# Attention and routed experts on one core: the attention part in a fixed order on every engine

## The chip, the cores and the metric

The kernel runs on one core of a Trainium2 chip. A core has several engines, each with its own stream of instructions: TensorE (PE, with its weight loads PEld), VectorE (DVE), ScalarE (ACT), GpSimd (POOL), and SyncE (SP), which here only issues transfers (DMA). An engine works through its stream in order; where an instruction needs what another engine or a transfer makes, it waits for a semaphore, and all that stands behind it in the same stream waits too.

The metric is the device time of a whole launch, in microseconds. The profile covers the span from the first to the last instruction of one execution, which is shorter than the launch.

## The reference

Two blocks follow one another. The first is attention over 4 batches, 8 heads, 768 positions and 64 features, with a mask: a query sees only keys whose 6 sign bits under a projection equal its own. The second sends each of the 3072 rows of 512 features to one of 8 experts, by cosine similarity, and gives gate times relu(x w1) w2.

```python
q_bits = (np.einsum('bhsd,dk->bhsk', q, proj) > 0)
k_bits = (np.einsum('bhsd,dk->bhsk', k, proj) > 0)
# buckets are the bits read as numbers
mask = q_bucket[:, :, :, None] == k_bucket[:, :, None, :]
scores = scale * np.matmul(q, k.transpose(0, 1, 3, 2))
scores = np.where(mask, scores, -1000000000.0)
attn = softmax(scores)
x = np.matmul(attn, v)            # then (B,H,S,D) -> (B*S, H*D)
...
logits = normed(x) @ normed(expert_emb).T / tau
expert_idx = np.argmax(logits, axis=1)
gate_w = softmax(logits)[expert_idx]
for e in range(E):
    h = np.maximum(x[mask_e] @ w1[e], 0.0)
    out[mask_e] = gate_w[mask_e, None] * (h @ w2[e])
```

## The kernel before

Attention works on 16 pairs of heads (4 batches of 4 pairs). A pair has 12 units: two halves s of the queries by 6 blocks c of keys. The loop takes three units at a time, so a pair is four steps, g = 0 to 3. A step makes the scores of three units and then the products with v of the three units before.

```python
def scores(u):
    ...
    ps = banks()                       # one of three PSUM buffers of two banks
    for h in range(2): nc.tensor.matmul(ps[:, h, 0:SH], lhsT=kt[...], rhs=qt[...], start=True, stop=False)
    for h in range(2): nc.tensor.matmul(ps[:, h, 0:SH], lhsT=kb[...], rhs=qb[...], start=False, stop=True)
    p = pts[u % NPT]                   # six buffers
    last[0] = nc.scalar.activation(p[:, :, 0:SH], ps[:, :, 0:SH], ACT.Exp, scale=ESCALE).ins
    if c == 1: ...                     # acc = p of unit 0 + p
    elif c > 1: last[1] = nc.vector.tensor_tensor(out=a[:], in0=a[:], in1=p[...], op=ALU.add).ins

def attend(u):                         # av += v^T p; after the last c:
    ...
    nc.scalar.copy(out=few[:], in_=ps[:, SH : SH + 1])
    nc.scalar.activation(xs(b)[:, j, ...], ps[:, 0:SH], ACT.Identity, bias=few[:])
```

The softmax's denominators of a pair are summed over partitions by TensorE (`sums`), go through DRAM twice to be laid out anew (za, zc, zd, rz), and are multiplied into x by GpSimd (`scale`). `store` writes x to DRAM, from where the expert part gathers rows; `add_squares` makes the norms; `prep_features` turns q and k, `prep_bits` makes the mask's features.

```python
def sums(pr):
    ps = banks()
    ...                                               # ones^T acc, eight matmuls
    nc.vector.tensor_scalar_add(z[:], ps[:, 0, 0:SH], TINY * S)
    nc.sync.dma_start(za[pr], z[0:P:32, :])
    nc.sync.dma_start(zc[:], za[pr]...)

def scale(pr):
    with tc.issue_after(last[1]):
        nc.vector.reciprocal(out=zc[:], in_=zc[:])
    nc.sync.dma_start(zd[pr]..., zc[:])
    for h in range(2): nc.sync.dma_start(rz[...], zd[pr]...)
    scaled[0] = nc.gpsimd.tensor_tensor(out=x, in0=x, in1=rz[...], op=ALU.mult).ins

def add_squares(pr, rp, ins):
    with tc.issue_after(ins):
        nc.scalar.activation(t[:], xs(b)[:, j], ACT.Square)
    if j > 0: nc.gpsimd.tensor_tensor(out=ssq[b][:], in0=ssq[b][:], in1=t[:], op=ALU.add)
```

The loop, with the order in which the program names the work. The framework then chooses each engine's order itself; `issue_after` and `high_priority` only steer it.

```python
for u0 in range(0, U + G, G):
    pr, g = u0 // PU, u0 % PU // G
    run(7 if pr == len(pairs) - 2 else 3)       # small steps of the placement of rows
    ...                                         # scores of three units
    if pr == len(pairs) - 2 and g == 3:
        lists(...); early = [fetch(src[0], pos[0], 0, 2, ZC + 1)]
    ...                                         # attend for the three units before
    if g == 0:
        prep_features(pr + 1, 0); add_squares(pr - 2, ...); sums(pr - 1); store(pr - 2)
        ...                                     # begin(b, ...) for the last batch but one
    elif g == 1:
        prep_features(pr + 1, 1)
        ...                                     # begin: counts for the placement
        scale(pr - 1)                           # in the last pair: behind the gathers
        ...                                     # last pair: fetch for the second expert
        square(pr)                              # sum of squares of q and k, for a bound check
        if j == 1 and b >= 0: lts[b] = logits(b, ...)
    elif g == 2:
        prep_bits(pr + 1); load(pr + 3)         # 8 loads of q and k, 1 of v
        ...                                     # fill, gates of the last batch but one
        if j == 1 and b >= 0: route(...)
    else:
        if pr == 2: prep_experts()              # loads, norms and turns the expert embeddings
        ...                                     # fill, gates
        if pr == 2 * NP:
            with tc.issue_after(loads[-1]): bring1(0, 0); bring2(0, 0)   # 2 MB each
early = [turn(got) for got in early]
store(len(pairs) - 2); scale_last(len(pairs) - 1); store(len(pairs) - 1)
...                                             # the bound check: largest square, turned and reduced
```

The expert part then begins with `hidden(0, early[0][0], 2 * P)`: 64 matmuls for rows of expert 0, in PSUM buffers that take the place of attention's.

Of the kernel before, what the change touches and what calls it, by code (L numbers as in the profile page):

```python
# [9 lines left out]
I32 = mybir.dt.int32  # L10
# [16 lines left out]
def kernel(  # L27
# [204 lines left out]
    def gates(b, rp):  # L232
        l, nrm = lts.pop(b)
        nc.vector.tensor_scalar_add(nrm[:], nrm[:], 1e-6)
        nc.vector.reciprocal(out=nrm[:], in_=nrm[:])
        nc.vector.tensor_tensor(out=l, in0=l, in1=nrm[:].unsqueeze(2).broadcast_to([P, NC, E]),
                                op=ALU.mult)
        nc.scalar.activation(l, l, ACT.Exp)
        g = rp.tile([P, NC], F32, name="g", tag="g")
        nc.vector.reduce_sum(out=g[:], in_=l, axis=AX.X)  # L240
        nc.vector.tensor_scalar_add(g[:], g[:], 1e-9)
        nc.vector.reciprocal(out=gate_all[:, b], in_=g[:])
        nc.sync.dma_start(gd[b * S : (b + 1) * S, :].rearrange("(p c) o -> p (c o)", c=NC), gate_all[:, b])
# [79 lines left out]
    def lists(slots, src, pos, n, ps, sp):  # L323
# [4 lines left out]
        nc.vector.tensor_scalar_add(src, tmp[:], float(N))  # L328
        for g in range(NQ):
            nc.tensor.matmul(ps[:, g * 2 * n : (g + 1) * 2 * n], lhsT=pick[:, g], rhs=half_[:].rearrange("p i t -> p (i t)"),  # L330
                             start=True, stop=True)
# [3 lines left out]
        return nc.vector.tensor_tensor(out=pos, in0=at[:], in1=t[:, :, :, 1], op=ALU.add).ins  # L335
# [11 lines left out]

    def bring2(i, e, **kw):
        nc.sync.dma_start(w2s[i][:], w2[bass.ds(e, 1)].rearrange("o (c p) m -> p (o c) m", p=P), **kw)

    xgs = [const.tile([P, NQ, P], F32, name=f"xg{i}") for i in range(4)]
    taken, copied = [0, 0, 0], [None]


    def fetch(src, pos, t, n, width=N + 1):
        parts = []
        for i in range(n):
            xg = xgs[taken[2] % len(xgs)]
            taken[2] += 1
            for g in range(NQ):  # L360
                copied[0] = nc.gpsimd.indirect_dma_start(  # L361
                    out=xg[:, g, :], out_offset=None, in_=xd[0 : width * NQ, :],
                    in_offset=bass.IndirectOffsetOnAxis(ap=pos[:, t + i, g : g + 1], axis=0)).ins
            parts.append(xg)
        tiles = []
        for i in range(n):
            g = ggs[taken[1] % len(ggs)]
            taken[1] += 1
            with tc.issue_after(copied[0]):
                nc.gpsimd.indirect_dma_start(out=g[:], out_offset=None, in_=gd[:, :],  # L370
                                             in_offset=bass.IndirectOffsetOnAxis(ap=src[:, t + i : t + i + 1], axis=0))
# [17 lines left out]
    def add_squares(pr, rp, ins):  # L389
# [4 lines left out]
        with tc.issue_after(ins):  # L394
            nc.scalar.activation(t[:], xs(b)[:, j], ACT.Square)
        if j > 0:
            return nc.gpsimd.tensor_tensor(out=ssq[b][:], in0=ssq[b][:], in1=t[:], op=ALU.add).ins
# [3 lines left out]

    with ExitStack() as at:
        ldp = pool("ldp", 3, at)
# [25 lines left out]


        def prep_experts():
            emb = const.tile([E, DM], F32, name="emb")
            nc.sync.dma_start(emb[:], expert_emb[:, :])
            tau_t = const.tile([E, 1], F32, name="tau_t")
            nc.sync.dma_start(tau_t[:], tau.unsqueeze(0).broadcast_to([E, 1]))
            sq = rp.tile([E, DM], F32, name="emb_sq", tag="junk", bufs=2)
            ss = const.tile([E, 1], F32, name="emb_ss")
            with tc.issue_after(last[0]):
                nc.scalar.activation(sq[:], emb[:], ACT.Square, accum_out=ss[:])
            nrm = const.tile([E, 1], F32, name="emb_nrm")  # L440
            nc.gpsimd.tensor_tensor(out=nrm[:], in0=ss[:], in1=half[0:E, 0:1], op=ALU.pow)
            nc.vector.tensor_scalar_add(nrm[:], nrm[:], 1e-6)
            nc.vector.reciprocal(out=nrm[:], in_=nrm[:])
            rtau = const.tile([E, 1], F32, name="rtau")
            nc.vector.reciprocal(out=rtau[:], in_=tau_t[:])
            nc.vector.tensor_scalar(out=emb[:], in0=emb[:], scalar1=nrm[:, 0:1], scalar2=rtau[:, 0:1],
                                    op0=ALU.mult, op1=ALU.mult)
            ps = banks()
            for d in range(ND):
                nc.tensor.transpose(ps[:, 0, d * E : (d + 1) * E], emb[:, d * P : (d + 1) * P], ident[0:E, 0:E])  # L450
            with tc.high_priority():
# [3 lines left out]
        def load(pr):  # L455
# [4 lines left out]
            vt = ldp.tile([P, 2, NC, D], F32, name="vt", tag="vt", bufs=3)  # L460
# [6 lines left out]
            loads.append(nc.sync.dma_start(vt[:], v[b, 2 * j : 2 * j + 2].rearrange("h (p c) d -> p h c d", c=NC)).ins)  # L467
# [10 lines left out]
        def square(pr):  # L478
            qk = ld[pr][0]
            sq = rp.tile([P, 2 * S], BF16, name="qksq", tag="junk", bufs=2)  # L480
            with tc.issue_after(last[0]):
                nc.scalar.activation(sq[:], qk[:].rearrange("p i n f -> p (i n f)"), ACT.Square,
                                     accum_out=squares[:, pr : pr + 1])
# [27 lines left out]
        def scores(u):  # L511
# [12 lines left out]
            last[0] = nc.scalar.activation(p[:, :, 0:SH], ps[:, :, 0:SH], ACT.Exp, scale=ESCALE).ins  # L524
# [4 lines left out]
            elif c > 1:  # L529
                a = acc[pr, s]  # L530
                last[1] = nc.vector.tensor_tensor(out=a[:], in0=a[:], in1=p[:, :, 0:SH], op=ALU.add).ins  # L531


        def spare(n):
            return last[2][:, SH + 1 : SH + 1 + n]

        def attend(u):
# [7 lines left out]
            if c == NC - 1:  # L545
# [4 lines left out]
                last[2] = av.pop((pr, s))  # L550
# [19 lines left out]
        def scale(pr):  # L570
            b, j = pairs[pr]
            zc = zcs.pop(pr)
            with tc.issue_after(last[1]):
                nc.vector.reciprocal(out=zc[:], in_=zc[:])
# [6 lines left out]
            scaled[0] = nc.gpsimd.tensor_tensor(out=x, in0=x, in1=rz[:].rearrange("p s n -> p (s n)"), op=ALU.mult).ins  # L581


        def store(pr):
            b, j = pairs[pr]
            t = op.tile([P, S], F32, name="xb", tag="xb")
            with tc.issue_after(last[1]):
                nc.vector.transpose(t[:], xs(b)[:, j])  # L588
# [6 lines left out]
        def scale_last(pr):  # L595
# [10 lines left out]
            for s in range(2):  # L606
# [3 lines left out]
                ins = nc.vector.tensor_tensor(out=z[:, s], in0=x, in1=x, op=ALU.mult).ins  # L610
            x = xs(b)[:, j - 1]
            with tc.issue_after(ins):
                nc.vector.tensor_tensor(out=t[:], in0=x, in1=x, op=ALU.mult)
                nc.vector.tensor_tensor(out=t[:], in0=t[:], in1=z[:].rearrange("p s n -> p (s n)"), op=ALU.add)
                nc.vector.tensor_tensor(out=ssq[b][:], in0=ssq[b][:], in1=t[:], op=ALU.add)

        last, loads, scaled = [None, None, None], [], [None]
        steps = []

        def run(n):  # L620
            for _ in range(n):
                if steps:
                    with tc.issue_after(last[1]):
                        if next(steps[0], None) is None:
                            steps.pop(0)

        def begin(b, ps):
            with tc.high_priority():
                count(b, ps[:, 0 : E * NC], ps[:, E * NC :])
                steps.append(place(b, ps.rearrange("p (t n) -> p t n", t=2), rp))  # L630
                next(steps[0])

        for pr in range(3):
            load(pr)
        for i in range(2):
# [3 lines left out]
        early = []  # L639
        for u0 in range(0, U + G, G):  # L640
            pr, g = u0 // PU, u0 % PU // G
            run(7 if pr == len(pairs) - 2 else 3)
# [418 lines left out]
```

## Time and profile before

The time is 872.76 us, the median of three launches (872.59 to 873.0). The profiled span is 818.3 us.

| | before |
|---|---|
| TensorE busy | 730.6 us (89%) |
| VectorE busy | 345.5 us (42%) |
| ScalarE busy | 267.8 us (33%) |
| GpSimd busy | 223.4 us (27%) |
| last matmul of attention ends | about 427 us |
| first matmul of the expert part | 438.94 us |

The page gives the busy share of each engine in 40 equal slices of the span. A digit is tenths, and 9 means 90% or more; PEclk is the clock that TensorE was granted, in tenths. In a list of waits, a line names the engine and the line of the program that waited, the one that it waited for, and then the total in microseconds, the number of times and the longest. In a timeline, a line gives start, length, engine, line, operation, output and inputs; what stands in brackets is the idle time before it and what ended that. An issue of a transfer has the engine SPq.

### The profile page before, as it was taken

The page shows a single profiled execution, that of the slowest core. Times are in us where ns is not written, and L with a number is a line of the kernel's source. Part 1 is how long each engine was busy: PE and PEld are TensorE (multiplying, and loading weights), DVE is VectorE, ACT ScalarE, POOL GpSimd, SP SyncE. Part 2 cuts the span into 40 slices and gives each one's busy share as a digit, 9 for nine tenths or more (in the row PEclk, how much of TensorE's full clock was granted, in tenths as well). Part 3 has the DMA queues.
Part 4 walks back from the last instruction along what each step waited for, and adds up shares of the span by engine and source line. Part 5 has one row for each costly group of instructions (what it writes and reads, how often), then busy time and mean ns, then how long its engine had stood idle before and what let it go on. Part 6 is the DMA issues. An engine that isn't in the chain of part 4 may idle for free.

```text
span 818.3 us, 9991 instructions
## 1 busy us (share of the span) xinstructions
PE 730.6 (89%) x3669; PEld 361.2 (44%) x3669; DVE 345.5 (42%) x664; ACT 267.8 (33%) x432; POOL 223.4 (27%) x222
## 2 busy tenths in 40 slices
PE   5997299898998999849865999999999999999993
PEld 2442143343443433314324576654545454545481
DVE  5765187688775787628555141151010101010100
ACT  3654176564565565535450111110101010101020
POOL 4000131101202102110443117777661522010051
PEclk9998599999999999978986999999999999999997
DMA  8313344335438234541325402944442433333340
GB/s 153 80 23 76 78 81 96 70 69 98 83 55 265 52 71 75 98 83 17 82 49 152 126 20 96 348 153 161 166 159 89 155 125 128 113 129 114 129 144 20
DMA packets 198075, 87.56 MB, mean 107 GB/s; under 512 B 171377, under 2 KB 179373, under 8 KB 198008
## 3 DMA queue, kind: packets, MB, share of 16 engines
q1 hardware_dynamic: 188312, 72.94, 34.6%
q0 software_dynamic: 6560, 13.41, 4.8%
q10 hardware_dynamic: 3136, 0.39, 0.3%
q8 instruction: 33, 0.54, 0.3%
q14 instruction: 34, 0.28, 0.1%
HBM read 82.31 MB, written 13.31 MB: 117 GB/s over the span
## 4 chain that ended last, share of the span: by engine, by line
PE 65%; DMA 9%; DVE 8%; issue 7%; POOL 4%; ACT 3%; SPq 2%; DVEq 0%; ACTq 0%; POOLq 0%
PE ps_h L867 21%; PE ps_y L875 20%; PE banks L518 9%; PE av L543 9%; DMA zd<-zc 4%; DVE acc L531 3%; DMA rz<-zd 3%; PE banks L521 2%; ACT p L524 2%; POOL xT L581 2%; PE banks L496 1%; POOL xg L361 1%; SPq L463 1%; SPq L578 1%; DVE kb L507 1%
## 5 line engine op out<-in xcount | busy, mean ns | idle before, releaser
L518 PE MATMUL banks<-qt,kt 64*128 64x384 f32 x768 | 174.2, 527 | 20.0 <-ACT p L524 9.6
L875 PE MATMUL ps_y<-w,ht 128*128 128x512 f32 x416 | 180.9, 593 | 0.0
L524 ACT ACTIVATE p<-banks 128x768 f32<-128x768 f32 x192 | 153.2, 811 | 78.9 <-PE banks L521 77.0
L869 ACT ACTIVATE ht<-ps_h 128x384 f32<-128x384 f32 (+2 forms) x96 | 38.6, 403 | 319.0 <-PE ps_h L867 317.6
L543 PE MATMUL av<-p,vt 128*64 128x385 f32 x768 | 142.4, 506 | 0.0
L531 DVE TENSOR_TENSOR acc<-acc,p 128x768 f32<-128x768 f32 x128 | 132.2, 1033 | 22.0 <-ACT p L524 11.7
L867 PE MATMUL ps_h<-xgt,w 128*128 128x384 f32 (+1 forms) x512 | 139.6, 434 | 0.0
L875 PEld LDWEIGHTS ps_y<-w,ht 128*128 128x128 f32 x416 | 78.5, 190 | 95.2 <-issue 93.3
L361 POOL DMA_INDIRECT xg<-xd,pos x96 | 93.2, 971 | 66.8 <-issue 25.0
L581 POOL TENSOR_TENSOR xT<-xT,rz 128x768 f32<-128x768 f32 x15 | 30.4, 2030 | 293.8 <-DMA rz<-zd 279.2
L867 PEld LDWEIGHTS ps_h<-xgt,w 128*128 128x128 f32 x512 | 87.4, 190 | 52.2 <-issue 2.9
L518 PEld LDWEIGHTS banks<-qt,kt 64*128 64x128 f32 x768 | 69.5, 195 | 92.4 <-issue 43.1
L543 PEld LDWEIGHTS av<-p,vt 128*64 128x64 f32 x768 | 50.8, 139 | 79.3 <-issue 78.3
L879 DVE TENSOR_SCALAR y<-ps_y,gg 128x512 f32<-128x512 f32 x26 | 19.3, 744 | 142.5 <-PE ps_y L875 140.1
L381 DVE STREAM_TRANSPOSE xgt<-xg 128x512 f32<-128x512 f32 x21 | 14.2, 699 | 139.7 <-PE ps_h L867 80.4
L521 PE MATMUL banks<-qb,kb 64*128 64x384 bf16 x384 | 67.2, 332 | 0.0
L880 POOL DMA_INDIRECT out_dram<-y,src x24 | 24.3, 1012 | 146.8 <-DVE y L879 104.8
L867 PE MATMUL ps_h<-xge,w 128*128 128x256 f32 (+1 forms) x256 | 45.8, 341 | 11.8 <-issue 11.8
L528 DVE TENSOR_TENSOR acc<-p,p 128x768 f32<-128x768 f32 x32 | 31.6, 988 | 40.8 <-ACT p L524 40.8
L867 PEld LDWEIGHTS ps_h<-xge,w 128*128 128x128 f32 x256 | 40.7, 199 | 16.9 <-issue 12.9
L521 PEld LDWEIGHTS <-kb 64*128 64x128 bf16 x384 | 20.8, 97 | 26.5 <-issue 3.0
L588 DVE STREAM_TRANSPOSE xb<-xT 128x768 f32<-128x768 f32 x16 | 15.6, 974 | 29.0 <-POOL xT L581 29.0
(241 smaller groups left out, 393.2 us busy)
## 6 DMA issues: line engine op xcount, KB each, us to landing
w<-in_moe_w_dram SPq DMA_DIRECT2D x24, 2048.0 KB
qk<-in_q_dram SPq DMA_DIRECT2D x64, 96.0 KB
vt<-in_v_dram SPq DMA_DIRECT2D x16, 384.0 KB
xd<-xb SPq DMA_DIRECT2D x64, 96.0 KB
qk<-in_k_dram SPq DMA_DIRECT2D x60, 96.0 KB
rz<-zd SPq DMA_DIRECT2D x30, 192.0 KB
xg<-xd,pos POOLq DMA_INDIRECT x96, 2.8
qk<-in_k_dram ACTq DMA_DIRECT2D x4, 96.0 KB
```

What stands on the lines that cost most here:

```text
L361: copied[0] = nc.gpsimd.indirect_dma_start(out=xg[:, g, :], out_offset=None, in_=xd[0 : width * NQ, :], in_offset=bass.IndirectOffsetOnAxi ...
L518: nc.tensor.matmul(ps[:, h, 0:SH], lhsT=kt[rows[h], c // HC, kc], rhs=qt[rows[h], s, :], start=True, stop=False)
L521: nc.tensor.matmul(ps[:, h, 0:SH], lhsT=kb[rows[h], c // HC, kc], rhs=qb[rows[h], s, :], start=False, stop=True)
L524: last[0] = nc.scalar.activation(p[:, :, 0:SH], ps[:, :, 0:SH], ACT.Exp, scale=ESCALE).ins
L528: nc.vector.tensor_tensor(out=a[:], in0=pts[(u - 1) % NPT][:, :, 0:SH], in1=p[:, :, 0:SH], op=ALU.add)
L531: last[1] = nc.vector.tensor_tensor(out=a[:], in0=a[:], in1=p[:, :, 0:SH], op=ALU.add).ins
L543: nc.tensor.matmul(ps[h * D : (h + 1) * D, 0 : SH + 1], lhsT=vt[:, h, c, :], rhs=p[:, h, 0 : SH + 1], start=(c == 0), stop=(c == NC - 1))
L581: scaled[0] = nc.gpsimd.tensor_tensor(out=x, in0=x, in1=rz[:].rearrange("p s n -> p (s n)"), op=ALU.mult).ins
L867: nc.tensor.matmul(ph[:, 0:n], lhsT=w1s[i][:, d, f * P : (f + 1) * P], rhs=xt[:, d, 0:n], start=(d == 0), stop=(d == ND - 1))
L869: nc.scalar.activation(ht[:, f, 0:n], ph[:, 0:n], ACT.Relu)
L875: done[0] = nc.tensor.matmul(py[:], lhsT=ht[:, f, j * P : (j + 1) * P], rhs=w2s[i][:, f, :], start=(f == 0), stop=(f == NF - 1)).ins
L880: nc.gpsimd.indirect_dma_start(out=out[:, :], out_offset=bass.IndirectOffsetOnAxis(ap=src, axis=0), in_=y[:], in_offset=None, bounds_check ...
```

## The change

Each engine's order in attention, and that of SP's transfers, becomes the order in which the program names the instructions. A helper chains every instruction to the one before it on the same engine, with a dependency that needs no semaphore. The hints to the framework's own ordering go.

```diff
+    def in_order(n):
+        behind = {}
+        for ins in nc.cur_bb.bb.instructions[n:]:
+            if ins.engine in behind:
+                tc.add_manual_dep(ins, behind[ins.engine].name, mybir.DependencyInfo(
+                    mybir.DependencyClass.NoSync, mybir.DependencyReason.DATA), reason="in_order")
+            behind[ins.engine] = ins
...
-            with tc.issue_after(last[1]):
-                nc.vector.reciprocal(out=zc[:], in_=zc[:])
+            nc.vector.reciprocal(out=zc[:], in_=zc[:])
...
-            vt = ldp.tile([P, 2, NC, D], F32, name="vt", tag="vt", bufs=3)
+            vt = ldp.tile([P, 2, NC, D], F32, name="vt", tag="vt", bufs=4)
```

The embeddings are loaded behind the first pair's loads and prepared in three parts. The first expert's weights come in eight pieces, one a pair from pair 4 on. `gates` is split in three parts, so that VectorE and ScalarE needn't wait for one another in place. `lists` is split in `lists` and `places`, and the bound check is made in the last pair. The reciprocals' transfers go ahead of the loads, which are issued a step earlier; x is stored two steps later; the squares of q and k are made a pair earlier.

```diff
+    def piece(n):
+        i, s = n // ND, n % ND
+        if i == 0: nc.sync.dma_start(w1s[0][:, s], w1[0, s * P : (s + 1) * P, :])
+        else: ...                                    # a quarter of w2
...
         for pr in range(3):
             load(pr)
+            if pr == 0:
+                nc.sync.dma_start(emb[:], expert_emb[:, :])
+                nc.sync.dma_start(tau_t[:], tau.unsqueeze(0).broadcast_to([E, 1]))
...
             if g == 0:
+                if pr > 0:
+                    sums(pr - 1)
+                if j == 2 and end:
+                    begin(b, banks()[:, 0, 0 : 2 * E * NC])
                 prep_features(pr + 1, 0)
-                ...                                  # add_squares, sums, store(pr - 2), begin
+                if pr > 1:
+                    add_squares(pr - 2, rp)
+                if pr == 2:
+                    prep_experts(1)
+                if j == 2 and b >= 0:
+                    gates(b, rp, 0)
             elif g == 1:
                 prep_features(pr + 1, 1)
+                if pr > 0:
+                    scale(pr - 1)
+                load(pr + 3)
+                if NP <= pr < NP + 2 * ND:
+                    piece(pr - NP)
...
                 if j == 1 and b >= 0:
                     lts[b] = logits(b, ssq[b], banks()[:, 0], rp)
-                square(pr)
+                if pr == 0:
+                    square(0)
+                square(pr + 1)
+                if j == 3 and end:
+                    for e in range(1, EARLY):
+                        early.append(fetch(src[0], pos[0], e * KT, 2, ZC + 1))
+                    bound(0)
+                if j == 2 and b >= 0:
+                    gates(b, rp, 1)
             elif g == 2:
                 prep_bits(pr + 1)
-                load(pr + 3)
+                if pr > 1:
+                    store(pr - 2)
...                                                  # run(99), fill, gates(b, rp, 2), bound(1)
+            else:
+                if pr == 1:
+                    prep_experts(0)
                 if pr == 2:
-                    prep_experts()
+                    prep_experts(2)
...                                                  # route moves here from g == 2; fill as before
-                if pr == 2 * NP:
-                    with tc.issue_after(loads[-1]):
-                        bring1(0, 0)
-                        bring2(0, 0)
+                if j == 3 and end:
+                    early[0] = turn(early[0])
-        with tc.issue_after(last[1]):
-            early = [turn(got) for got in early]
         store(len(pairs) - 2)
         scale_last(len(pairs) - 1)
         store(len(pairs) - 1)
+        in_order(begun)
```

At the start of the expert part, the rows of the second expert are turned behind the first hidden layer:

```diff
         hidden(0, early[0][0], 2 * P)
+        early[1:] = [turn(got) for got in early[1:]]
         lt = logits(b, ssq[b], ps_x(), sp)
```

The arithmetic is the same but for the embeddings' scale, where one reciprocal of the norm times tau takes the place of two reciprocals.

## The prediction

> **What bounds the kernel now.** I read the page's 40 slices first, to see where TensorE is not full.
>
> ```profile
> PE   5997299898998999849865999999999999999993
> DVE  5765187688775787628555141151010101010100
> PEclk9998599999999999978986999999999999999997
> ```
>
> A slice is 20.5 us. From the 23rd slice (about 440 us) to the end TensorE is full at full clock: that is the expert part. Before it lies attention, with holes (the 5th slice has a 2) and with a lower granted clock at just those slices. VectorE never has a 9. So attention is not held by an engine that is always busy; something keeps interrupting TensorE. Busy time by stretches says how much: TensorE was busy 365.8 us of the first 440 us, so it was idle 74 us. Next, the waits of the whole span, longest in total first.
>
> ```profile
> POOL xT L581 <- DMA rz<-zd: 279.2, 13, 53.8
> ...
> ACT xsq L395 <- POOL xT L581: 30.8, 7, 10.1
> ...
> PE banks L450 <- DVE emb L446: 15.7, 1, 15.7
> ...
> PE ps_h L867 <- issue: 11.8, 1, 11.8
> ...
> PE banks L192 <- POOL xT L581: 9.9, 2, 8.9
> ...
> PE banks L518 <- ACT p L524: 9.6, 4, 4.3
> ...
> PE banks L518 <- DVE z L563: 8.0, 4, 3.9
> ```
>
> GpSimd's multiplication by the reciprocals waits for the transfer rz; ACT's square of its result and TensorE's logits wait for GpSimd; the exponentials behind that square then hold up the scores. The waits of SP's own queue show what makes rz late.
>
> ```profile
> SPq L575 <- DVE zc L574: 100.6, 13, 14.7
> SPq L578 <- DMA zd<-zc: 31.4, 14, 3.2
> ```
>
> SP stood 100.6 us before the store of the reciprocals, because VectorE reached the reciprocal late. One example from the timeline, a window around 220 us:
>
> ```profile
> 217.66 0.85 PE L560 MATMUL banks<-acc,ones 128*32 128x384 f32 x8
> ...
> 224.86 0.36 SPq L566 DMA_DIRECT2D zc<-za  x1
> ...
> 237.48 0.19 DVE L574 RECIPROCAL zc<-zc 128x12 f32<-128x12 f32 x1
> ...
> 240.42 1.28 SPq L578 DMA_DIRECT2D rz<-zd  x2
> ...
> 245.02 1.80 POOL L581 TENSOR_TENSOR xT<-xT,rz 128x768 f32<-128x768 f32 x1 [19.48 <-DMA rz<-zd]
> 246.86 0.84 ACT L395 ACTIVATE xsq<-xT 128x768 f32<-128x768 f32 x1 [3.62 <-POOL xT L581]
> ```
>
> The sums of a pair of heads are made at 217.66 and their product with x only at 245.02, 27 us later; 12.6 us of that lie between the issue of zc and the reciprocal, 0.19 us long. Elsewhere zc was issued at 127.15 and the store behind its reciprocal at 129.35, so the transfer needs about 2 us and the rest is VectorE's order.
>
> The yardstick is the distance between the sums (L560) of successive pairs, from the timeline of TensorE: 20.45, 44.72, 20.45, 22.16, 25.75, 21.67, 26.71, 21.25, 29.02, 23.14, 23.20, 21.18, 42.09, 24.50 us, from 35.75 to 402.04. A pair with nothing in its way takes 20.45 us, which also comes out of its parts: four steps of 4.71 (three units: scores 2.62, values 2.09), bits 0.81, sums 0.78. Fourteen such pairs are 286.3 us; they took 366.3.
>
> [...] the granted clock was 0.64 and 0.51 in the stretches 80 to 90 and 90 to 100 us, after the wait of 15.7 us, and twelve value matmuls that took 2.09 us elsewhere took 3.64 us at 69 us. So a hole costs more than its length. [...] an acc addition took 1.69 us while the product at 116.84 ran, against a median of 0.958. [...]
>
> **The change part by part.**
>
> (1) *Expert embeddings.* Their loads go out with those of the first pair, and the preparation is spread over pairs 1 and 2. Before, the load was issued at 90.77 and TensorE waited 15.7 us, then ran slowly. The interval with it is 44.72, so 24.3 over a clean one; that interval also holds the 3.9 us wait for an exponential at 63 to 67 us and its slow matmuls (12 at 3.64 for 2.09). All of it should go, save 0.6 us for the transposes: -23.
>
> (2) *Reciprocal chain in hand order.* From the start of sums(n), with durations of this trace: z ends at +1.4 (0.85 of matmul, 0.55 on VectorE), za is issued at +1.5, zc 1.7 later (125.46 to 127.15), and lands by +5.3. In the new order VectorE reaches the reciprocal after the three additions and the transpose of kt of the next step, about +6.5, so it waits for nothing. zd goes at +6.6, rz 2 to 4 later (184.56 after 182.21; 133.39 after 129.35), lands 4 later, GpSimd needs 1.8: done at +15 to +17, against +29 in the example. ACT's square is now at about +19.5, one pair later: 3 to 5 us of slack. The waits of ACT and of the logits (30.8 and 9.9 us) should vanish.
>
> (3) *SP's queue.* Per pair it now has za, zc, zd, rz twice, nine loads at about 0.66, a piece, four stores of x. Issue time: 0.56 + 0.37 + 0.38 + 1.29 + 6.0 + 0.5 + 2.1 = 11.2 us, and waits of about 1.3 for za and 2 to 4 for zd: 14 to 17 of 20.45. As rz goes before the loads and the square that frees qk is made a pair earlier, no load waits for a buffer; the fourth vt buffer does the same for v. SP fits, with some 3 us to spare.
>
> (4) *Weights in pieces.* The two loads of 2 MB at 247 us (DMA share 1.01 in 250 to 260) become eight of 0.5 MB; za at 248.55 took 3.92 us to issue behind them and zc was issued only at 262.50. That pair took 29.02. Expected: -5 of its 8.6 excess.
>
> (5) *Routing, gates and stores spread.* VectorE's total hardly changes. Summed over the stretches of 20 us it was busy some 279 us in attention, which is 17 a pair or 83 to 85% of 20.45. It can follow, but with little room in the pairs with the placement: sum some 6 us there, in pieces now. I allow 1 us for each of eight such pairs and 3 us for the crowded pair 14 (placement of seven steps at a time, fill, lists, gates): +11. TensorE's own routing work remains: logits 1.5 + 0.5, transposes, counts, fills, about 3.3 us for each of three batches: +10.
>
> So fourteen intervals become 286.3 + 10 + 11 = 307, against 366: **-59**. Parts 1 and 4 are inside this.
>
> (6) *Last pair and hand-over.* From the last sums to the last pair's own sums took 402.04 to 425.48; in it TensorE waited 4.3 us for an exponential behind the square of pair 13's product, which began only at 409.47, after eight gathers on GpSimd. That product now stands ahead of the gathers: -3. Then TensorE stood 11.8 us until 438.94. The reader of the PSUM that the expert part takes over, VectorE's maximum for the bound check (438.61, 0.23), stood behind a transpose that waited 9.7 us for gathers. The change does the check in the last pair and that transpose after the first hidden layer. Some 1.5 us remain for the last ACT copies: **-10**. With no hole there, the first 64 hidden matmuls lose part of their slow start, 16.86 against 13.97 for those of the second expert: **-2**.
>
> (7) *Start.* The two squares in pair 0 and the embedding load before pair 1's loads may hold VectorE for a moment: **+1**.
>
> Sum: -59 - 3 - 10 - 2 + 1 = -73. The expert part itself, 367 us from 438.94 to the end, keeps its instructions and its bound; its second weights are issued some 14 us after attention but needed only 33 us after. The measured time is 54 us above the span; I take this as fixed. 872.76 - 73 = 799.8; since two allowances are guesses on the careful side I say **797 us**.
>
> **The rivals.** *VectorE becomes the bound.* For it: 83% busy on average, in-order waits (about 1.5 us for the bits, 0.5 for the sums in each pair)[...]. Against it: before, TensorE kept 20.45 in the pair from 100.92 to 121.37, where everything but routing ran. If it holds, pairs run at 22 to 23 and the gain falls to about 50: 822. *SP becomes the bound,* or one late transfer now stops everything behind it, because no scheduler fills holes any more. For it: 14 to 17 us of 20.45 are taken[...]. Against it: nothing on SP is needed sooner than 3 us after its slot. Then the reciprocals slip again and ACT waits: 815 to 835. *All stalls vanish:* 286 + 10 and no allowance: 786. *Hidden anyway:* that the removed waits lay off the path is refuted by TensorE's idle 74 us and the intervals.
>
> **Range and chances.** 776 to 826 holds rivals one to three in their milder forms. For no gain over 2% some 56 us of the 73 would have to come back: I give faster 0.94, within 2% 0.04, slower 0.02.
>
> **What would show it.** Right: intervals of sums of 20.5 to 23 throughout, none over 26; TensorE idle under 25 us in attention and clock near 1.00 there; reciprocal within 8 us of its sums; no wait of ACT's square for GpSimd; the expert part starting within 3 us of the last sums, at about 365 us; weights no burst. Wrong: VectorE at 95% with scores waiting for z or the bits (rival one); SP's waits before zd or za growing from pair to pair (rival two); or the expert part longer than 367 us because its weights or gathers come too late.

## The result, and the profile after

| | before | after |
|---|---|---|
| launch, median (range) | 872.88 us (872.59 to 875.61) | 829.15 us (826.14 to 833.59) |
| span of the profiled execution | 818.3 us | 826.0 us |
| first sums of a pair | 35.75 us | 38.04 us |
| first matmul of the expert part | 438.94 us | 387.70 us |

The ratio after to before is 0.950, with a 95% interval of 0.945 to 0.955: 43.7 us are gained, where 73 to 76 were predicted. The table holds a contradiction that carries this study. The expert part begins 51 us earlier, and yet the profiled span became longer. Either the expert part got slower, or the two profiles do not show the same thing.

First the slices of the changed kernel (40 slices of 20.65 us, tenths of busy time; PEclk is TensorE's granted clock):

```profile
PE   4999999989998999794998113999999999999993
DVE  4777887887789787855241100031100101010000
PEclk9999999999999999896999555999999999999997
```

Attention is now nearly full. The 2 of the fifth slice is gone, and the clock stays at 9 up to an 8 at 330 us and a 6 at 372 us. But from the 23rd to the 25th slice (454 to 516 us), inside the expert part, TensorE shows 1, 1 and 3 at half clock. The profile of before had a 9 at every slice there.

Of the waits of the whole span (total, times, longest), these answer to the list of before:

```profile
ACT ht L908 <- PE ps_h L906: 257.1, 80, 24.2
POOL xT L603 <- DMA rz<-zd: 235.4, 15, 42.7
...
ACT ht L908 <- remote: 76.9, 5, 24.6
...
PE ps_h L906 <- issue: 48.8, 3, 19.7
...
PE banks L622 <- DVE acc L554: 9.9, 1, 9.9
...
PE banks L541 <- DVE z L586: 6.5, 3, 2.9
```

GpSimd still waits for rz, but now no engine waits for GpSimd's products: the waits of ACT's square and of the logits for its product are gone. In their place stand two that were not predicted. TensorE waits 9.9 us for VectorE before the last sums. And in the expert part ScalarE waits for something called "remote" and TensorE for nothing that the profile shows ("issue"), three times and 48.8 us in all.

SP's own waits that answer to those of before:

```profile
SPq L600 <- DMA zd<-zc: 45.8, 15, 3.9
...
SPq L597 <- DVE zc L596: 30.1, 10, 5.9
```

The wait for the reciprocal fell from 100.6 to 30.1 us. The chain of one pair, from the timeline around 220 us:

```profile
211.57 0.85 PE L583 MATMUL banks<-acc,ones 128*32 128x384 f32 x8
...
217.87 0.38 SPq L589 DMA_DIRECT2D zc<-za  x1
...
219.72 0.23 DVE L596 RECIPROCAL zc<-zc 128x12 f32<-128x12 f32 x1 [0.80 <-DMA zc<-za]
...
223.12 1.29 SPq L600 DMA_DIRECT2D rz<-zd  x2
...
227.57 1.84 POOL L603 TENSOR_TENSOR xT<-xT,rz 128x768 f32<-128x768 f32 x1 [12.48 <-DMA rz<-zd]
```

From the sums to the end of the product it now takes 17.8 us and not 29.2, and the square of this product comes only at 235.40, 6 us later.

The distance between the sums of successive pairs, from TensorE's timeline, is now 20.45, 21.15, 20.45, 20.44, 23.05, 20.76, 26.79, 20.44, 23.04, 20.60, 26.70, 20.45, 23.04 and 30.39 us: 317.75 in all, against 366.3 before and 307 predicted.

The hand-over, TensorE and VectorE:

```profile
374.44 0.81 PE L622 MATMUL banks<-acc,ones 128*64 128x384 f32 x4
385.19 1.55 PE L622 MATMUL banks<-acc,ones 128*64 128x384 f32 x4 [9.93 <-DVE acc L554]
387.70 12.56 PE L906 MATMUL ps_h<-xge,w 128*128 128x256 f32 x45 [0.97 <-ACT zl L625]
```

```profile
378.30 0.71 DVE L395 STREAM_TRANSPOSE xge<-xg 128x512 f32<-128x512 f32 x1 [6.33 <-DMA xg<-xd,pos]
378.93 0.92 DVE L554 TENSOR_TENSOR acc<-acc,p 128x768 f32<-128x768 f32 x1
383.58 0.71 DVE L395 STREAM_TRANSPOSE xge<-xg 128x512 f32<-128x512 f32 x1 [3.73 <-DMA xg<-xd,pos]
384.22 0.92 DVE L554 TENSOR_TENSOR acc<-acc,p 128x768 f32<-128x768 f32 x1
```

Before each of the last two additions of the last pair stands a transpose of the *second* expert's rows, which waits for its gathers, 6.33 and 3.73 us. Nothing needs these rows before the second hidden layer, at 420.27. They are named behind the part that the change puts in order, so the framework was free to place them, and put them in front of what TensorE waits for.

Last, ScalarE in the expert part, the relu of the hidden layer, where the first tile of 128 rows begins:

```profile
434.75 0.38 ACT L908 ACTIVATE ht<-ps_h 128x256 f32<-128x256 f32 x1 [1.34 <-issue]
461.30 0.28 ACT L908 ACTIVATE ht<-ps_h 128x128 f32<-128x128 f32 x1 [26.17 <-issue]
483.04 0.28 ACT L908 ACTIVATE ht<-ps_h 128x128 f32<-128x128 f32 x1 [21.46 <-remote]
504.73 0.28 ACT L908 ACTIVATE ht<-ps_h 128x128 f32<-128x128 f32 x1 [21.42 <-remote]
511.05 0.79 ACT L908 ACTIVATE ht<-ps_h 128x128 f32<-128x128 f32 x4 [6.04 <-remote]
```

TensorE had finished four groups by 452.1 and stood, since all four PSUM buffers were full. ScalarE learned of them one at a time, 21.7 us apart. The counter of TensorE's semaphore, as the trace has it, moves at 482.95, 504.65, 510.97, 511.06, 511.16 and 511.25: two at the slow pace and then the backlog, 0.09 us apart. Meanwhile GpSimd issued 56 gathers and stores in an unbroken run, one each 1.26 us, from 432.2 to 502.65; the backlog came 8.3 us after the end of its last issue. VectorE and ScalarE had next to nothing to do: from 460 to 500 us they were busy 4.19 and 0.56 us, and the clock granted to TensorE was 0.50.

### The profile page after: what moved, and what is told of

It is laid out like the page before. It is cut to its first block, busy times and chain, and to the rows that moved or that the text cites. A ratio compares the mean times of both kernels' runs of the same rounds, so it can differ in the third digit from the quotient of the medians.

```text
span 826.0 us, 10015 instructions
## 1 busy us (share of the span) xinstructions
PE 723.6 (88%) x3669; PEld 360.4 (44%) x3669; DVE 357.7 (43%) x664; ACT 268.2 (32%) x432; POOL 221.7 (27%) x222
## 4 chain that ended last, share of the span: by engine, by line
PE 39%; another core or an unknown queue 6%; issue 5%; POOL 1%; ACT 0%; POOLq 0%; ACTq 0%
PE ps_h L906 20%; PE ps_y L914 18%; POOL xg L376 1%; POOL out_dram L919 0%; ACT ht L908 0%; PE ps_x L192 0%; POOL gg L384 0%; PE ps_x L981 0%; PE ps_x L200 0%; PE ps_x L322 0%; ACTq L908 0%; PE ps_x L337 0%; POOLq L1054 0%; POOLq L919 0%
## 5 line engine op out<-in xcount | busy, mean ns | idle before, releaser
L541 PE MATMUL banks<-qt,kt 64*128 64x384 f32 x768 | 166.1, 510 | 8.4 <-DVE z L586 6.5
L554 DVE TENSOR_TENSOR acc<-acc,p 128x768 f32<-128x768 f32 x128 | 139.7, 1092 | 13.4 <-issue 1.7
L541 PEld LDWEIGHTS banks<-qt,kt 64*128 64x128 f32 x768 | 65.7, 189 | 74.0 <-issue 39.8
L906 PE MATMUL ps_h<-xge,w 128*128 128x256 f32 (+1 forms) x256 | 50.3, 361 | 54.0 <-issue 48.8
L906 PEld LDWEIGHTS ps_h<-xge,w 128*128 128x128 f32 x256 | 44.1, 215 | 61.2 <-issue 50.5
L544 PE MATMUL banks<-qb,kb 64*128 64x384 bf16 x384 | 64.4, 325 | 0.3 <-DVE kb L530 0.3
L410 POOL TENSOR_TENSOR ssq__163<-ssq__163,xsq 128x768 f32<-128x768 f32 x10 | 18.8, 1876 | 43.7 <-ACT xsq L408 43.7
```

The source lines that it names most:

```text
L541: nc.tensor.matmul(ps[:, h, 0:SH], lhsT=kt[rows[h], c // HC, kc], rhs=qt[rows[h], s, :], start=True, stop=False)
L544: nc.tensor.matmul(ps[:, h, 0:SH], lhsT=kb[rows[h], c // HC, kc], rhs=qb[rows[h], s, :], start=False, stop=True)
L906: nc.tensor.matmul(ph[:, 0:n], lhsT=w1s[i][:, d, f * P : (f + 1) * P], rhs=xt[:, d, 0:n], start=(d == 0), stop=(d == ND - 1))
```

## The experiments

Two questions followed: is the stall the change's doing, and where did the rest go. Each group below ran on one chip beside the kernel before, and the median of that is given with it.

**1. The kernels again, the turn in its place, the gathers in another order.** `before_again` and `after_again` are the two kernels unchanged. `turn_last` holds the second expert's turn behind VectorE's last transpose of x:

```diff
-        early[1:] = [turn(got) for got in early[1:]]
+        with tc.issue_after(turned_x[0]):       # the last transpose in store()
+            early[1:] = [turn(got) for got in early[1:]]
```

`gg_behind` is the changed kernel with the gathers of the gates behind those of the rows, the order they had before:

```diff
+            with tc.issue_after(copied[0]):     # the last gather of rows
                 nc.gpsimd.indirect_dma_start(out=g[:], ..., in_=gd[:, :], ...)
```

Expected of the four, in this order:

> The kernel before, unchanged. Its times (872.6 to 875.6) lie 52 us above its profiled execution (820.25), while the changed kernel's profiled execution (827.93) is like its times (826 to 834). Theory A: the 62 us in which the changed kernel's ScalarE waits for results of TensorE that are long there (434.7 to 511 us, in steps of 21.5) belong to the change, and the kernel before has no such wait: a new profile of it shows none, spans near 818, and the 52 us are something outside of the span. Theory B: such a wait comes in executions of both kernels, and the profile of before merely caught one without it: spans near 870, and in a new profile steps of about 21.5 us near the first late tiles.

> The changed kernel, unchanged. Both theories: 826 to 834 again if the wait of 62 us comes every time. If it comes by chance, some executions should be near 766 (828 less 62), and the wait in another place or number of steps.

> The changed kernel with the turn of the second expert's first rows held behind attention's last transpose on VectorE. Theory: the framework put that turn, which lies outside the fixed order, between the last two additions of the denominators, where it waited for gathers (6.3 and 3.7 us) and TensorE's last sums waited 9.9 us. Then this kernel starts the expert part 8 to 10 us earlier and the time falls by as much, to about 819, if the wait of 62 us stays as it is. Rival: the additions wait for something else, and nothing moves.

> The changed kernel with the gathers of the gates issued behind those of the rows again, as before the change; GpSimd's order in the burst of gathers is then that of the kernel before. Theory A1: the burst's new order (four gate gathers first) makes the wait of 62 us; it should go, 766. Theory B: the order has nothing to do with it, 826 to 834 with the same steps.

Measured, with the kernel before at 879.44 us:

| | us | ratio to before (95%) |
|---|---|---|
| before_again | 880.65 | 1.000 (0.998 to 1.003) |
| after_again | 833.77 | 0.947 (0.945 to 0.950) |
| turn_last | 815.65 | 0.926 (0.924 to 0.929) |
| gg_behind | 829.79 | 0.942 (0.938 to 0.945) |

Here the profile of the unchanged kernel has the same stall. Its busy times by stretches (columns PE, PEld, DVE, ACT, POOL, each in us with its count, then clock, DMA share, GB/s), first of this execution and then of the one profiled at the start:

```profile
500.00:520.00 20.00, 9.17 (x54) 7.16 (x52) 2.79 (x5) 0.56 (x2) 15.12 (x17) 0.80 0.20 59
520.00:540.00 20.00, 1.43 (x6) 1.43 (x7) 2.11 (x3) 0.28 (x1) 15.30 (x16) 0.50 0.19 53
540.00:560.00 20.00, 0.66 (x4) 0.35 (x2) 0.71 (x1) 0.04 (x1) 14.31 (x15) 0.50 0.18 49
```

```profile
500.00:520.00 20.00, 20.00 (x137) 16.17 (x136) 2.59 (x4) 3.90 (x14) 15.12 (x17) 1.00 0.65 216
520.00:540.00 20.00, 20.00 (x65) 11.27 (x64) 3.94 (x6) 2.52 (x6) 15.32 (x16) 1.00 0.86 313
```

Same program, same 15 us of gathers in 20 on GpSimd; TensorE full in one and all but empty in the other. The spans are 879.3 and 818.3, and 58.7 of these 61 us lie in the expert part, from its first matmul to the end (438.1 and 379.4). So the stall is not the change's doing, and the launch is only 1.8 us longer than its span (881.12 and 879.3): the "54 us above the span" were this stall, which the profile on the page did not happen to contain: that execution had itself taken only 820.25 us. The order of the gathers is not its cause: `gg_behind` stalls as well.

`turn_last` gains 18 us on `after_again`, where 8 to 10 had been expected. TensorE at its hand-over:

```profile
371.23 4.10 PE L567 MATMUL av<-p,vt 128*64 128x385 f32 x24
375.16 1.46 PE L623 MATMUL banks<-acc,ones 128*64 128x384 f32 x8
377.59 14.08 PE L907 MATMUL ps_h<-xge,w 128*128 128x256 f32 x64 [0.97 <-ACT zl L626]
```

The eight last sums run together, the expert part starts at 377.59 where `after_again` has 392.98, and its first 64 matmuls take 14.08 us, where `after_again` needs 16.90; the granted clock was 1.00 from 380 to 400 us, and 0.66 in `after_again`. Some 14 us are the turn's: TensorE had stood 10.8 us between the two halves of the last sums, and the expert part is 2.9 shorter. Another 5 lie in pair 15 ahead of them, where TensorE in `after_again` waited 3.05 us for exponentials, under gathers, and was granted a clock of 0.83 from 360 to 380 us, where `turn_last` has 1.00. Two lines of program, some 14 of the missing 30 us.

**2. Breaking up the run of gathers.** GpSimd fetches the rows of later experts as far ahead as its buffers go. In `paced`, on top of `turn_last`, the gathers for each expert after the first full one read their positions from a copy, which VectorE makes behind the last output of the expert two before. `held` does so for the first full expert too. `after_held` and `before_held` are the changed kernel and the one before with the same hold.

```diff
+        def tiles_later(e):
+            with tc.issue_after(turned[0]):     # the latest output, y
+                nc.vector.tensor_copy(out=pos_l[:, e * KT : (e + 1) * KT], in_=pos[1][:, e * KT : (e + 1) * KT])
+            return fetch(src[1], pos_l[:], e * KT, KT)
...
-                nxt = turn(tiles_of(e + 1, 0))
+                nxt = turn(tiles_later(e + 1))
```

> turn_last, with the gathers for the third full expert and all later ones held behind the last output of the expert two before (their positions are copied on VectorE behind that output). Only the gathers of the late tiles and of the first full expert (10 + 15 issues of 1.26 us) can still run under the late tiles. Theory (a long unbroken run of GpSimd gathers holds back TensorE's semaphore updates; the stall ends some 10 us after the run ends): the run ends near 461 us instead of 489, TensorE is at work again near 470 instead of 496, the time falls from 816 to about 788 us. Rival 1 (the stall belongs to the first matmul groups of 128 columns and their activations, whatever GpSimd does): the three waits of about 20 us of the activations stay, 812 to 822 us. Rival 2 (the stall is a fixed backlog of three updates of 20 us): the same as rival 1.

> As paced, and the gathers of the first full expert are held too, behind the output of the first late tile; no gather is left to issue under the first late tile's first layer. Theory: no activation waits 20 us, TensorE passes through the late tiles with under 10 us of idle time and waits at most 10 us for the held gathers; the stall of 62 us goes and 755 to 770 us are left. Rivals: the three waits of about 20 us stay, and the held gathers add up to 10 us: 815 to 830 us.

> The changed kernel as it is (with its misplaced turn) and the gathers held as in held. Theory: the stall of about 60 us goes, about 775 to 785 us. Rivals: 830 to 845 us.

> The kernel before with the gathers held as in held. Theory: its stall of about 55 us goes as well, 820 to 832 us, near the 818.3 us of the one execution without the stall; the change is then worth about 50 us between this and the changed kernel held the same way, and about 65 us with the turn in its place. Rivals: 875 to 890 us.

Measured: `paced` 753.59, `held` 764.24, `after_held` 779.66, `before_held` 830.48. But the unpaced kernel before took 819.72 us on this chip (818.07 to 822.12, seven runs), not 879: there was no stall to remove. These four tell nothing of its cause, and without the surprise in the control they would have been read as proof. What they do show is the price of holding: `before_held` is 1.4% slower than before (1.010 to 1.018), since TensorE waits some 9 us for the held gathers.

**3. The same kernels on a chip without the stall.** Four of them ran again.

> The changed kernel, unchanged, once more beside the paced ones. The unchanged kernel before took 820 us where the gathers were held, and 880 us beside the first runs: the stall comes on some chips and not on others. Where the kernel before takes about 820 us: the changed kernel has no stall either and takes 768 to 780 us. Where it takes about 875 to 880 us: 826 to 834 us as measured.

> Where the kernel before takes about 820 us: 752 to 762 us (815.7 less the stall of about 60). Where it takes about 880 us: 814 to 817 us as before.

> Where the kernel before takes about 880 us, so that the stall is there: the theory of the run of gathers makes this 780 to 795 us (the run ends near 461 us in place of 489), the rivals (the stall belongs to the first matmul groups of 128 columns, or is a fixed backlog) 812 to 822 us. Where it takes about 820 us: 752 to 756 us, as the first time, and nothing is told apart.

> Where the kernel before takes about 880 us: the theory of the run of gathers makes this 760 to 770 us, as where there is no stall; the rivals 820 to 830 us. Where it takes about 820 us: 762 to 766 us, as the first time.

The kernel before took 817.85 us: again no stall. The changed kernel then takes 769.08 (ratio 0.938, 0.934 to 0.943), `turn_last_c` 753.82 (0.922, 0.918 to 0.925), `paced_c` 754.92, `held_c` 763.91. So the stall costs the kernel before and the changed one about the same, 60 us or so, and without it the change brings 48.8 us: still 24 short. Of these `turn_last_c` brings 15.3. For the rest, the traces point to the last interval of 30 us. TensorE's timeline of `turn_last_c` there:

```profile
341.20 0.33 PE L545 MATMUL banks<-qb,kb 64*128 64x384 bf16 x2
345.49 0.32 PE L337 MATMUL banks<-half__3125,pick 128*128 128x48 bf16 x4 [3.96 <-DVE half__3125 L329]
345.74 4.12 PE L567 MATMUL av<-p,vt 128*64 128x385 f32 x12
```

TensorE stands 3.96 us at the matmuls that turn the first expert's list into positions. VectorE is behind with the bits of pair 15, a transpose of x and the gates, all named before. Then the value products take 4.12 us where 12 of them took 2.16 at 334 us; the granted clock of 340 to 350 us is 0.69. With the slow products the hole of 4 us costs 5.9 (3.96 + 4.12 - 2.16).

**4. Those matmuls one block later.** `spread` is `turn_last` with them behind the first value products of pair 15:

```diff
-            if end and j == 2 and g == 3:
-                places(listed, pos[0][:], NS, banks()[:, 0], rp)
-                early = [fetch(src[0], pos[0], 0, 2, ZC + 1)]
             for u in range(u0 - G, u0):
                 if 0 <= u < U:
                     attend(u)
+            if end and j == 3 and g == 0:
+                places(...); early = [fetch(...)]          # unchanged
```

> turn_last, with the matmuls that turn the first expert's lists into positions moved from pair 14 to the next pair, one group of blocks later on TensorE. In the traces TensorE waits there 4 us for VectorE (3.96 us at half_), the clock then drops (0.69 in that stretch) and the next group of av matmuls takes 4.12 us in place of 2.16; the interval between the sums of pairs 13 and 14 is 30.3 us and not 20.5 to 23. Theory (crowding on VectorE, paid once on TensorE in order): 5 to 7 us less than turn_last: ratio to the kernel before 0.913 to 0.916 where that takes 820 us, 0.919 to 0.921 where it takes 880. Rival (VectorE itself is full there, so the wait only moves to the next block sums): within 2 us of turn_last, ratio 0.920 to 0.924 (820) or 0.925 to 0.927 (880).

> spread with the gathers held as in held. Where the kernel before takes about 880 us (the stall is there): the theory of the long run of gathers makes this about 755 us, 45 to 55 us less than spread; the rivals (the stall belongs to the first 128-column groups or is a fixed backlog) make it 8 to 12 us more than spread, about 820. Where the kernel before takes about 820 us: about 10 us more than spread, 755 to 759, by the wait for the held gathers.

`spread` takes 749.26 us with the kernel before at 820.53 (0.911, 0.906 to 0.916), the fastest of all and 71.3 us under the kernel before. The last interval is 23.71 us instead of 30.07. In the same stretch, first `turn_last_c` and then `spread`:

```profile
340.00:350.00 10.00, 5.95 (x28) 2.13 (x26) 8.76 (x21) 2.02 (x3) 2.27 (x2) 0.69 0.41 81
```

```profile
340.00:350.00 10.00, 9.90 (x70) 4.02 (x68) 9.45 (x22) 6.03 (x9) 1.81 (x1) 1.00 0.42 81
```

VectorE is as busy as ever (9.45 of 10), and TensorE no longer waits for it. The crowding was real, and it cost time only because one matmul in TensorE's fixed order depended on it. About 4.6 us come through to the end (753.82 and 749.26, on two chips). `spread_held`, 760.84 where 755 to 759 had been expected, again had no stall to meet.

**5. The stall, met at last.** `spread_paced` is `spread` with the pacing of `paced`.

> spread with the gathers for the third full expert and later held behind the last output of the expert two before, as in paced. Where the kernel before takes about 880 us: the theory of the run of gathers makes this 770 to 790 us (the stall shortened to about half, as the run ends near 455 us), the rivals 808 to 818. Where the kernel before takes about 820 us: 748 to 751, as spread, since nothing waits for these gathers.

It took 778.54 us where the kernel before took 873.71, inside what the run of gathers foretold and 30 us under the rivals. Without an unpaced kernel beside it this was one leg only, so all three went to one chip:

> The control, unpaced. Where the kernel before takes about 875 to 880 us: 805 to 813 us, TensorE losing some 52 us in the stall as in the four earlier traces of it, until about 9 us after the last of the run of some 56 gathers. Where the kernel before takes about 820 us: 748 to 751 us.

> Where the kernel before takes about 875 to 880 us: 776 to 782 us, TensorE losing 18 us, until 7 to 9 us after the 26th gather, the last of the shorter run. Where it takes about 820 us: 748 to 752 us, as spread_b.

> Where the kernel before takes about 875 to 880 us: if the run of gathers is what the stall needs, 756 to 766 us, under 5 us of the stall left beside the 9 us of waiting for the held gathers; if the first 128-column groups stall under any gathers near them, 775 us or more. Where it takes about 820 us: 757 to 762 us, as the first time.

Measured, with the kernel before at 874.92. The last two columns are counted from the traces; idle is that of TensorE in the stall:

| | us | ratio (95%) | unbroken run on GpSimd | idle |
|---|---|---|---|---|
| spread_b | 814.52 | 0.932 (0.930 to 0.934) | 56 issues, 417.6 to 488.1 | 53.1 us |
| spread_paced_b | 778.42 | 0.891 (0.889 to 0.894) | 26 issues, 418.1 to 450.6 | 18.1 us |
| spread_held_b | 765.84 | 0.875 (0.873 to 0.878) | 12 issues, 422.9 to 437.7 | none; 6.7 us for the held rows |

ScalarE in `spread_paced_b` and then in `spread_held_b`:

```profile
420.57 0.38 ACT L909 ACTIVATE ht<-ps_h 128x256 f32<-128x256 f32 x1 [1.34 <-issue]
454.92 0.28 ACT L909 ACTIVATE ht<-ps_h 128x128 f32<-128x128 f32 x1 [33.96 <-remote]
457.77 0.79 ACT L909 ACTIVATE ht<-ps_h 128x128 f32<-128x128 f32 x4 [2.58 <-PE ps_h L907]
```

```profile
440.18 0.28 ACT L909 ACTIVATE ht<-ps_h 128x128 f32<-128x128 f32 x1 [14.43 <-PE ps_h L907]
441.08 0.28 ACT L909 ACTIVATE ht<-ps_h 128x128 f32<-128x128 f32 x1 [0.62 <-PE ps_h L907]
```

The backlog came 8.4 us after the end of the run in `spread_b` (488.1 to 496.50), 7.2 us after it in `spread_paced_b` (450.6 to 457.77) and 8.3 in the changed kernel's first profile. With no gathers under the first groups, in `spread_held_b`, the stall does not begin: 0.9 us from one relu to the next, as on chips without the stall. The rivals, that it belongs to the first groups of 128 columns or is a fixed backlog, fall. `spread_held_b` beats `spread_b` by 48.7 us here and loses to it by 11.6 on the chip without the stall (760.84 and 749.26).

The hold takes away TensorE's standing, not the lateness. In the eleven traces without the stall, no relu of the expert part starts more than 0.4 us after the end of its last matmul. In `spread_held_b` relus are up to 6.3 us late under the later runs of 14 gathers. But a group of 384 columns takes 2.58 us there, so four buffers hold 10.3 us of TensorE's work, where groups of 128 columns at 0.9 us fill them in 3.6.

`spread_b` was slower than its expectation (805 to 813), and its trace shows the same lateness once more. The gathers of the first expert now run under pair 15, and VectorE waits for a TensorE result there:

```profile
364.45 0.28 DVE L663 TENSOR_REDUCE beyond<-banks 1x1 f32<-1x128 f32 x1 [3.08 <-remote]
```

The matmul that it reads had ended at 358.80, 5.6 us earlier, and TensorE then stands 4.2 us for VectorE. In `spread` on the chip without the stall the same reduction follows its matmul by 0.6 us. So even under a run of ten gathers a result came late; what `spread` gains in pair 14 it gives back here.

## Why the prediction was right or wrong

**Wrong in size: 829 and not 797, by two of its steps; a third premise was false and by luck did little harm.** The comparison that its sum was about is that of the executions without the stall: spans 818.3 before and 767.1 after, 51.2 us, where it said 73. The difference of 21.8 us divides into 10.8 + 8.5 - 0.9 + 2.0 + 1.2 + 0.2, in the order of the next paragraphs, all from these two traces. The launches add 7.6 us: what lies above these spans is 54.5 us before and 62.0 after (829.15 - 767.1). And 797 itself was 2.8 under the sum, 799.8.

*Step 5, the allowances for VectorE and TensorE's routing:* fourteen intervals were to be 307 and are 318 in `after_c`: 11 us. Where nothing is crowded they are 20.45 to 21.15, as said, and the three with the logits' matmuls are 23.04. The excess sits in three others, 26.9, 26.8 and 30.3, together 22.6 us of 31.8. I allowed 1 us for VectorE in each of eight pairs and 3 in the crowded pair 14, beside TensorE's own routing. Pair 14 took 9.9: in the changed kernel's first profile TensorE stands 3.71 us there, then is granted half its clock (0.50 from 345.20 to 352.00 us), and 12 value products take 4.12 us and not 2.16. `spread` showed 6.4 us of that interval to be just the place of one group of matmuls. The other two took 6.4 and 6.3, by the same kind of wait. The changed kernel's profile, in the first of them:

```profile
171.09 1.65 PE L541 MATMUL banks<-qt,kt 64*128 64x384 f32 x4 [2.92 <-DVE z L586]
...
172.99 2.89 PE L566 MATMUL av<-p,vt 128*64 128x385 f32 x12
```

Here z ends 6.7 us after the start of its sums, and not 1.4 as step 2 has it: steps of the placement of rows stand before it in VectorE's fixed order. The value products behind the wait take 2.89 us, where 12 of them take 2.16; the granted clock was 0.50 from 171.10 to 174.50 us. The other interval has the same wait of 2.92 us. Before the change the two were 26.71 and 23.20, so in the second the fixed order lost 3.6 us to the framework's. This is read from the traces; no run moved z.

*Step 6, the last pair and the hand-over:* from the last interval's end to the last pair's own sums I said 23.4 - 3 = 20.4 us; it took 28.9, so 8.5 lost. The sentence that failed is "that transpose after the first hidden layer". I took the program's order for the order that runs, but the chain covers only what stands inside attention, and this line stands behind it. `turn_last` shows it: 15.3 us back without the stall, 18.1 with it, and in both some 14 are the turn's by the traces. The hand-over proper went as said, from 13.5 to 2.5 us (I said 10 less, so 0.9 gained). The 2 us for the slow start did not come: in the changed kernel's first profile the granted clock behind the wait was 0.50 (387.70 to 392.90 us), and the 64 matmuls took 16.66 us. With the turn in place they took 14.08, against 16.86 before.

*Step 7, the start:* +2.2 and not +1. *The expert part itself* keeps its length: 379.6 us from its first matmul to the end, against 379.4 (the "367 us" of the prediction is a slip: 818.3 - 438.94 is 379.4).

*"54 us above the span; I take this as fixed."* This is the false premise. The gap was a stall in the expert part that the profiled execution lacked. It happens to cost both kernels about the same (before: 53 to 62 us between chips, after: 60 to 65), so the difference survived. Had the change moved the gathers, as `spread_held` does, the prediction would have been wrong by the whole of it.

**Right:** step 1, embeddings: the second interval fell from 44.72 to 21.15, 23.6 for the 23 said. Step 2: the reciprocal 8.2 us after its sums (6.5 in the working, 8 at most), the product done at 17.8 (15 to 17), both a little late, no wait of ACT's square for GpSimd. Step 3: SP does keep up; the wait of rz for zd is 3.05 us a pair (2 to 4). Step 4: the pair with the burst of weights went from 29.02 to 23.04, 6 for 5. TensorE's idle time from the first sums to 402 us is 24.7 us, where I had said under 25. Two of the signs failed: three intervals are over 26, and the expert part starts at 387.7 and not at about 365. Of the rivals none came: neither VectorE nor SP became the bound. What came was a piece of the first one, crowding in three pairs, and an ordering fault that no rival named. With the turn and pair 14 mended, `spread` gains 71.3 us on its chip, near the 73 of the sum; partly because its last pair took 17.9 us and not 20.4.

**Open:** why some chips stall and others don't. Chips numbered 8 and 15 had it each time, 1 and 3 never, in all later runs of the kernel before; the chip of the first runs isn't on record. Nor do the runs show why TensorE's results come late while GpSimd issues gathers.

## What to carry to other kernels

An order laid out by hand ends where its range ends: look in the trace at the first instructions behind it, on the engine that it made critical. When the launch is tens of microseconds longer than the profiled span, don't call that fixed; profile again, until a span and a time belong to the same execution. And where the trace shows TensorE standing under a long run of gathers on GpSimd, break the run up (`spread_paced_b` took 778.42 us beside 814.52 of `spread_b`), and no more strictly than needed: without the stall, `paced_c` took 754.92 us beside 753.82 of `turn_last_c`, no clear loss, and `held_c` 763.91. Before a fix for a stall is believed, the control beside it must show the stall.

## What the runs showed of the hardware

On two chips of four, while GpSimd issued indirect transfers without a break (one each 1.26 us), results of TensorE reached ScalarE and VectorE late: by 5.6 us under a run of ten, and one per 20 to 22 us under a run of 56, with the backlog 0.09 us apart once the run was over. Four full PSUM buffers turned this into 49 to 53 us of a standing TensorE. In the changed kernel's first profile four groups of matmuls had ended by 452.1 us, and the update that ScalarE's second relu followed is recorded at 482.95, 30.8 us later. No run here shows what happened between the two.
